# Moving the x tiles ahead in the first loads of a fused attention-and-MLP kernel, and reordering its first Q projection to match

## The chip, the cores and the metric

One core of one Trainium2 chip. The metric is the device time of one execution in microseconds (us); the profile's span, from the first to the last recorded instruction, is about 1.7 us shorter.

## The reference

For `x` of 2048 tokens by 512 dims, the output is `g * a + (1 - g) * b`:

```python
g = sigmoid((x * gate_w).sum(-1))
q, k, v = split(x @ wqkv)            # 32 heads of 16; a: attention over 8 keys, 2 tokens apart
a = softmax(q . k_gathered / 4) @ v_gathered @ wo
b = (gelu(layernorm(x).T @ w1 + b1) @ w2 + b2).T
```

Only the first piece of the projection `x @ wqkv` matters here: Q of the first 512 tokens ("Q block 0"), the first thing that TensorE can do when data arrives.

## The kernel before

The kernel lists its operations, and a static scheduler puts them in an order per engine from its own estimates. Two orders are fixed by hand: that of the loads on each of two DMA queues (the SP queue and the ACT queue), and that of TensorE's operations. Both are touched.

A tile of x is 128 tokens by 512 dims (128 KB). It must be transposed before the projection can use it: TensorE transposes 128 x 128 pieces into PSUM, and VectorE (tiles 0 and 2) or ScalarE (tiles 1 and 3) copies them back. `k_` counts halves of the dims: half 0 is dims 0-255, half 1 is dims 256-511. A block `Wq_dt` holds Wq's 128 rows for dims `128*dt` and up, also 128 KB.

```python
xld = {}
for k_ in (0, 2):
    xld[k_] = xq(k_, "sp")           # load of x tile k_
    xq(k_ + 1, "act")
    wqq(k_, "sp")                    # load of block k_ of Wq
    wqq(k_ + 1, "act")
for k_ in range(2):                  # Wk in two halves, issued when x tile 0 has landed
    load("wk%d" % k_, ..., deps=[xld[0]])
ld_w("wv", 2, 0, 4, "wv")
# ... (cut: x tiles 4-15, small vectors, W1)

PE(f_warm, 2.6, [], ["b7"], "warm")  # 5 matmuls of 512 and 4 of 128 columns on constants

def f_q0(hb, dt):                    # step dt of Q block 0; hb 0: tokens 0-255, 1: 256-511, 2: all 512
    c0, c1 = ((0, 256), (256, 512), (0, 512))[hb]
    # ... (cut: four matmuls, one per bank, accumulating over dt)

def pe_tx(t):                        # transposes of tiles t and t+1
    for k_ in range(2):
        for t_ in (t, t + 1):
            PE(f_tx(t_, k_), ...)    # 2 transposes, then the copy back
            xt_ev(t_, k_)

pe_tx(0)
pe_q0(0, 0)
pe_q0(0, 1)
pe_tx(2)
pe_q0(0, 2)
pe_q0(1, 0)
pe_q0(1, 1)
pe_q0(1, 2)
pe_q0(2, 3)
# ... (cut: the K, V and Q projections, attention, MLP)
```

Of the kernel before, what the change touches and what calls it, by code (L numbers as in the profile page):

```python
# [307 lines left out]
def bass_gated_mix__sliding_local_dilated__mixer_token_mlp__prompt_kernel(nc, A_x, A_wqkv, A_wo, B_x, B_w1, B_b1, B_w2, B_b2, gate_w, out, dbg=None):  # L308
    with contextlib.ExitStack() as es:
# [201 lines left out]
        def ld_first(name, dst, src, nbytes, res, queue):  # L511
            return load(name, dst, src, nbytes, res, queue=queue)

        def xq(t, queue):
            return ld_first("x%d" % t, X[:, t:t + 1, :], xv[:, t:t + 1, :], 131072, ["x%d" % t], queue)

        def wqq(k_, queue):
            return ld_first("wq%d" % k_, WQKV[:, k_:k_ + 1, 0:D], wqkv_v[:, k_:k_ + 1, 0:D], 131072, ["wq%d" % k_], queue)

        xld = {}  # L520
        for k_ in (0, 2):
            xld[k_] = xq(k_, "sp")
            xq(k_ + 1, "act")
            wqq(k_, "sp")
            wqq(k_ + 1, "act")
        for k_ in range(2):
            load("wk%d" % k_, WQKV[:, 2 * k_:2 * k_ + 2, D:2 * D], wqkv_v[:, 2 * k_:2 * k_ + 2, D:2 * D], 2 * 128 * D * 2, ["wk%d" % k_], deps=[xld[0]])
        ld_w("wv", 2, 0, 4, "wv")
# [27 lines left out]
        def PE(fn, dur, reads, writes, name, prio=0):  # L556
            op = A("pe", fn, dur, reads=reads, writes=writes, after=([chain[0]] if chain[0] is not None else []), name=name, prio=prio)
            chain[0] = op
            return op
# [3 lines left out]
        def f_tx(t, k_):  # L563
            def fn(e):
                ins = None
                for d_ in range(2):
                    ins = e.transpose(out=psb(4 + 2 * (t % 2) + k_)[:, d_ * 128:d_ * 128 + 128],  # L567
                                      in_=X[:, t, (2 * k_ + d_) * 128:(2 * k_ + d_ + 1) * 128], identity=IDENT)
                return ins
            return fn  # L570
# [3 lines left out]
        def xt_ev(t, k_):  # L574
            eng = ("dve", "act")[t % 2]
            bk = 4 + 2 * (t % 2) + k_
            src = sub(psb(bk), 0, [(128, 2), (1, 128)])
            dst = sub(XT, 2 * k_ * S + t * 128, [(S, 2), (1, 128)])
            extl[eng] = A(eng, (lambda e: e.tensor_copy(out=dst, in_=src)) if eng == "dve" else act(dst, src, AF.Copy),  # L579
                          0.27 if eng == "dve" else 0.35, reads=["b%d" % bk], writes=["xt0_%d_%d" % (t, k_)], name="ext%d_%d" % (t, k_), prio=-30)  # L580

        def f_q0(hb, dt):
            c0, c1 = ((0, 256), (256, 512), (0, 512))[hb]

            def fn(e):
                ins = None
                for dl in range(4):
                    ins = e.matmul(ps[:, dl, c0:c1], lhsT=sub(WQKV, dt * 3 * D + dl, [(4, 128)]),  # L588
                                   rhs=XT[:, dt, c0:c1], start=(dt == 0 and hb == 0), stop=(dt == 3), skip_group_check=True)
                return ins  # L590
            return fn

        def pe_tx(t):
            for k_ in range(2):
                for t_ in (t, t + 1):
                    PE(f_tx(t_, k_), 0.2, ["x%d" % t_, "ident"], ["b%d" % (4 + 2 * (t_ % 2) + k_)], "tx%d_%d" % (t_, k_))
                    xt_ev(t_, k_)

        def pe_q0(hb, dt):
            PE(f_q0(hb, dt), 0.87 if hb == 2 else 0.44, ["xt0_%d_%d" % (t_, dt // 2) for t_ in ((0, 1), (2, 3), (0, 1, 2, 3))[hb]] + ["wq%d" % dt], ["b%d" % dl for dl in range(4)],  # L600
               "q0_%d_%d" % (hb, dt))
# [3 lines left out]

        pe_tx(0)
        pe_q0(0, 0)
        pe_q0(0, 1)
        pe_tx(2)
        pe_q0(0, 2)  # L610
        pe_q0(1, 0)
        pe_q0(1, 1)
        pe_q0(1, 2)
        pe_q0(2, 3)
        XT0 = ["xt0_%d_%d" % (t, k_) for t in range(4) for k_ in range(2)]

# [402 lines left out]
```

## Time and profile before

| | before |
|---|---|
| median of the first 3 runs | 165.76 us |
| span of the profiled run | 163.9 us |
| TensorE busy | 159.3 us (97%) |
| TensorE in the chain that ended last | 95% |
| first K projection | 9.46 us |
| from there to the end | 154.4 us |

"First K projection" is the start of the first matmul after Q block 0, and it ends what I call the head. Some matmul records are missing from a trace; where that one is, I take the start of its weight load plus the 0.21 us that separate the two elsewhere.

The page of the kernel before, parts 1 and 4: busy time by engine, and the chain of work that ended last, followed back from the last instruction.

```profile
PE 159.3 (97%) x793; PEld 77.5 (47%) x808; DVE 150.7 (92%) x126; ACT 70.2 (43%) x100; POOL 12.0 (7%) x36
...
PE 95%; DMA 2%; ACT 1%; issue 1%; DVE 0%
PE ps L858 29%; PE ps L885 29%; PE ps L649 23%; PE ps L894 8%; PE ps L588 3%; DMA arena<-in_A_x_dram 2%; PE ps L722 1%; ACT arena L453 1%; PE ps L567 1%; PE ps L717 1%; DVE arena L579 0%; PE ps L604 0%
```

TensorE is the chain, and behind the head it has no gaps worth naming. So a change in the head is worth exactly what it moves the first K projection, as long as nothing later is late.

The timeline of the kernel before, TensorE alone, 3 to 10.3 us (start, length, instructions; L551 is the warm-up, L567 the transposes, L588 Q block 0, L649 the projections after it):

```profile
start us, us, engine line op out<-in xcount [idle before <-releaser]
2.51 1.06 PE L551 MATMUL ps<-const-bfloat16-1.0 128*128 128x512 bf16 x5
3.74 1.01 PE L567 MATMUL ps<-arena 128*128 128x128 bf16 x8 [0.17 <-DMA arena<-in_A_x_dram]
4.89 1.61 PE L588 MATMUL ps<-arena 128*128 128x256 bf16 x8
6.33 0.61 PE L567 MATMUL ps<-arena 128*128 128x128 bf16 x8
6.78 2.84 PE L588 MATMUL ps<-arena 128*128 128x256 bf16 x19
9.46 1.03 PE L649 MATMUL ps<-arena 128*128 128x512 bf16 x4
```

Only the first load, x tile 0, makes TensorE wait. The transposes of tiles 2-3 follow the eighth Q matmul without a gap, at 6.33 us; by then their loads have landed. The first eight Q matmuls run slower than the later ones: start to start they are 0.213 us apart until about 6.1 us and 0.110 us after it. That is the clock of TensorE's array going from half to full speed. The Trainium skill ("TensorE: Matmul & The Clock Gate", Part 1) gives N / 1.2 GHz start to start while cold, and the 0.213 us for 256 columns agree.

When each load has landed is read from its semaphore in the trace, which counts to 16 (to 0.01 us). The loads go out in pairs, one on each queue, and land in pairs:

| place | before: SP, ACT | landed, us | after: SP, ACT | landed, us |
|---|---|---|---|---|
| first | x0, x1 | 3.60, 3.80 | x0, x1 | 3.48, 3.67 |
| second | Wq0, Wq1 | 4.25, 4.42 | Wq0, x2 | 4.10, 4.28 |
| third | x2, x3 | 5.91, 6.23 | Wq1, x3 | 6.25, 6.47 |
| fourth | Wq2, Wq3 | 6.65, 6.81 | Wq3, Wq2 | 6.97, 7.18 |

### The profile page before, as it was taken

To read this page: it belongs to the slowest core of one execution; us is meant where nothing else is said; L and a number is where in the kernel's file an instruction comes from. 1 tells how busy PE (TensorE), PEld (TensorE's weight loads), DVE (VectorE), ACT (ScalarE), POOL (GpSimd) and SP (SyncE) were. 2 spreads that over 40 slices of the span, in tenths; PEclk is the share of its full clock that TensorE was granted. 3 is DMA by queue.
4 is the path that set the end of the run, shared out by engine and by line. 5 is a ranking of instruction groups with operands and counts; after the bars stand their busy time and mean duration, and the time that the engine had idled before them with its cause. 6 is when DMAs were issued, how large, how long until landed. Compare 5 with 4: busy or idle time off the path is not lost.

```text
span 163.9 us, 1989 instructions
## 1 busy us (share of the span) xinstructions
PE 159.3 (97%) x793; PEld 77.5 (47%) x808; DVE 150.7 (92%) x126; ACT 70.2 (43%) x100; POOL 12.0 (7%) x36
## 2 busy tenths in 40 slices
PE   7999999999999999999999999999999999999993
PEld 3755555555544444444444344444444444444641
DVE  0589989999999999999999999999999999999971
ACT  3357677766672379753111258111121111111164
POOL 3000021020000000004000000002200222000000
DMA  4999969909499094999998974990998799991014
GB/s 153 288 233 253 254 128 291 199 11 188 91 304 308 1 247 120 256 290 290 298 263 233 270 203 142 298 232 10 283 254 192 185 204 201 211 222 38 32 58 135
DMA packets 44684, 32.24 MB, mean 197 GB/s; under 512 B 7940, under 2 KB 42244, under 8 KB 44676
## 3 DMA queue, kind: packets, MB, share of 16 engines
q1 hardware_dynamic: 41444, 22.06, 51.9%
q0 software_dynamic: 2512, 9.44, 27.2%
q10 hardware_dynamic: 720, 0.62, 1.1%
q8 instruction: 6, 0.10, 0.2%
q14 instruction: 2, 0.02, 0.0%
HBM read 18.88 MB, written 2.10 MB: 128 GB/s over the span
## 4 chain that ended last, share of the span: by engine, by line
PE 95%; DMA 2%; ACT 1%; issue 1%; DVE 0%
PE ps L858 29%; PE ps L885 29%; PE ps L649 23%; PE ps L894 8%; PE ps L588 3%; DMA arena<-in_A_x_dram 2%; PE ps L722 1%; ACT arena L453 1%; PE ps L567 1%; PE ps L717 1%; DVE arena L579 0%; PE ps L604 0%
## 5 line engine op out<-in xcount | busy, mean ns | idle before, releaser
L450 DVE TENSOR_TENSOR arena<-arena 128x4096 bf16<-128x4096 bf16 (+8 forms) x79 | 132.0, 1718 | 1.9 <-ACT arena L453 0.6
L885 PE MATMUL ps<-arena 128*128 128x512 bf16 (+2 forms) x234 | 50.0, 366 | 0.2
L858 PE MATMUL ps<-arena 128*128 128x512 bf16 x218 | 48.5, 379 | 0.3
L453 ACT ACTIVATE arena<-ps,arena 128x512 bf16<-128x512 f32 (+1 forms) x30 | 21.8, 731 | 60.7 <-PE ps L894 37.7
L453 ACT ACTIVATE arena<-ps 128x512 bf16<-128x512 f32 (+3 forms) x53 | 32.9, 629 | 18.3 <-PE ps L649 10.9
L649 PE MATMUL ps<-arena 128*128 128x512 bf16 x173 | 38.0, 379 | 0.2
L885 PEld LDWEIGHTS ps<-arena 128*128 128x128 bf16 x238 | 22.8, 98 | 25.9
L858 PEld LDWEIGHTS ps<-arena 128*128 128x128 bf16 x224 | 21.7, 98 | 26.8 <-issue 0.8
L649 PEld LDWEIGHTS ps<-arena 128*128 128x128 bf16 x176 | 19.9, 113 | 18.0
L894 PE MATMUL ps<-arena 128*128 128x512 bf16 (+2 forms) x67 | 15.6, 366 | 0.1
L453 ACT ACTIVATE arena<-arena 128x16 f32<-128x16 f32 (+5 forms) x10 | 6.7, 678 | 9.7 <-DVE arena L450 9.7
L692 DVE BATCH_NORM_STATS2 arena<-arena 128x6 f32<-128x512 bf16 x16 | 9.9, 679 | 0.5 <-DMA arena<-in_A_x_dram 0.5
L954 ACT ACT_TABLE_LOAD x7 | 9.0, 1283 | 2.8 <-issue 2.7
L894 PEld LDWEIGHTS ps<-arena 128*128 128x128 bf16 x68 | 6.5, 98 | 7.3
L790 POOL DMA_DIRECT2D arena<-arena x8 | 4.3, 556 | 75.2 <-DVE arena L450 75.2
L706 DVE TENSOR_SCALAR arena<-arena 128x512 bf16<-128x512 bf16 x16 | 5.3, 406 | 0.0
L579 DVE COPY arena<-ps 128x256 bf16<-128x256 bf16 x4 | 1.1, 291 | 4.4 <-PE ps L567 4.2
L827 POOL DMA_DIRECT2D arena<-arena x3 | 3.6, 1209 | 17.7 <-DVE arena L450 17.7
L747 POOL DMA_DIRECT2D arena<-arena x2 | 2.5, 1268 | 31.5 <-DVE arena L692 21.5
L588 PE MATMUL ps<-arena 128*128 128x256 bf16 (+1 forms) x27 | 4.4, 313 | 0.2
L588 PEld LDWEIGHTS ps<-arena 128*128 128x128 bf16 x28 | 3.1, 119 | 1.1 <-DVE arena L579 0.4
L551 PE MATMUL ps<-const-bfloat16-1.0 128*128 128x512 bf16 (+1 forms) x9 | 2.7, 483 | 0.8 <-PEq L1004 0.8
(30 smaller groups left out, 14.4 us busy)
## 6 DMA issues: line engine op xcount, KB each, us to landing
arena<-in_B_w_dram SPq DMA_DIRECT2D x7, 1024.0 KB, 6.5
arena<-in_B_w_dram SPq DMA_DIRECT2D x8, 896.0 KB, 9.9
arena<-arena POOLq DMA_DIRECT2D x5, 1024.0 KB, 10.0
arena<-arena POOLq DMA_DIRECT2D x8, 512.0 KB, 11.7
out_dram<-arena SPq DMA_DIRECT2D x15, 128.0 KB, 2.3
arena<-in_A_x_dram SPq DMA_DIRECT2D x3, 512.0 KB, 4.7
arena<-in_A_wqkv_dram SPq DMA_DIRECT2D x2, 256.0 KB, 4.3
arena<-in_A_wqkv_dram SPq DMA_DIRECT2D x1, 512.0 KB, 6.5
```

The source lines that it names most:

```text
L450: return lambda e: e.tensor_tensor(out=o_, in0=a_, in1=b_, op=op_)
L453: return lambda e: e.activation(out=o_, in_=i_, func=f_, **kw)
L588: ins = e.matmul(ps[:, dl, c0:c1], lhsT=sub(WQKV, dt * 3 * D + dl, [(4, 128)]), rhs=XT[:, dt, c0:c1], start=(dt == 0 and hb == 0), stop=(d ...
L649: ins = e.matmul(ps[:, bank, :], lhsT=sub(WQKV, dt * 3 * D + tn * D + dl, [(4, 128)]), rhs=XT[:, dt, sb * 512:(sb + 1) * 512], start=(dt = ...
L692: A("dve", (lambda t_: lambda e: e.bn_stats(out=ST6[:, t_, :], in_=X[:, t_, :]))(t), 0.67, reads=["x%d" % t], writes=["st%d" % t], name="s ...
L706: A("dve", (lambda t_: lambda e: e.tensor_scalar(out=X[:, t_, :], in0=X[:, t_, :], scalar1=col(RSTD, t_), scalar2=col(NMR, t_), op0=ALU.mu ...
L790: prev = sch.dma("pool", (lambda d_, s_: lambda e: e.dma_start(d_, s_))(dst, src), 524288, sch.dsem("av%d_%d" % (h, c)), issue=1.0, reads= ...
L827: sch.dma("pool", (lambda o_, i_: lambda e: e.dma_start(o_, i_, accum_op=ALU.add, max_dma_last_dim=4096))(pw(0, 4), pw(4, 4)), 1800000, sc ...
L858: ins = e.matmul(ps[:, bank, :], lhsT=W1H[ft // 2][:, st, 128 * (ft % 2):128 * (ft % 2) + 128], rhs=X[:, st, :], start=(st == 0), stop=(st ...
L885: ins = e.matmul(ps[:, bank, 0:c1 - c0], lhsT=W2S[i // 2][:, ft, 128 * (i % 2):128 * (i % 2) + 128], rhs=UT[:, ft, c0:c1], start=(ft == 0) ...
L894: ins = e.matmul(ps[:, bank, 0:c1 - c0], lhsT=OT[:, i // 2, dl, 128 * (i % 2):128 * (i % 2) + 128], rhs=WO[:, dl, c0:c1], start=False, sto ...
L954: e.preload_act_table_set(want)
```

## The change

The intent is to have the x tiles early, so that the transposes of tiles 2-3 can follow Wq0's first step at once, and to do the last two steps (dims 256-511) in one go for all 512 tokens, with wider and fewer matmuls.

```diff
         xld = {}
-        for k_ in (0, 2):
-            xld[k_] = xq(k_, "sp")
-            xq(k_ + 1, "act")
+        for k_ in range(4):
+            xld[k_] = xq(k_, "sp" if k_ == 0 else "act")
+        for k_ in (0, 1, 3):
             wqq(k_, "sp")
-            wqq(k_ + 1, "act")
+        wqq(2, "act")
...
         pe_tx(0)
         pe_q0(0, 0)
+        pe_tx(2)
         pe_q0(0, 1)
-        pe_tx(2)
-        pe_q0(0, 2)
         pe_q0(1, 0)
         pe_q0(1, 1)
-        pe_q0(1, 2)
+        pe_q0(2, 2)
         pe_q0(2, 3)
```

## The prediction

> **What bounds the kernel.** TensorE. In the chain that ended last PE is 95%, unbroken from 3.74 us (first transpose, released by x tile 0) to about 160.4 us. VectorE (92%) follows PE's start: its first long product waits for a K eviction. It finishes its last attention output at 158.7 us and PE uses that from 159.35 us (timeline): about 0.6 us of room. So a change in the head is worth what it moves the first K projection, now at 9.46 us.
>
> **The head now** (timeline and landings by semaphore). x0 lands at 3.61, x1 3.80, Wq0 4.25, Wq1 4.43, x2 5.91, x3 6.23, Wq2 6.65, Wq3 6.81, Wk0 7.46 us. PE: transposes of tiles 0-1 3.74 to about 4.55; a hole of about 0.35 us for the evictions (DVE 0.29, ACT 0.38 us); eight 256-column matmuls from 4.90, the first five or six at 213 ns start to start, later ones at 110; transposes of tiles 2-3 from 6.34 at 56 ns each; then sixteen 256-column matmuls, with one hole of about 0.07 us for an eviction; four of 512 at 216 ns. The 213 ns are the half clock: the Trainium skill, "TensorE: Matmul & The Clock Gate", Part 1, gives exactly N/1.2 GHz start to start when cold, and says the window is free-running. This trace agrees (256/1.2 = 213), with the change at about 6.05 us.
>
> **What the change does.** Matmuls: 24 of 256 and 4 of 512 columns become 16 and 8. Eight steps of 110 ns become four of 216, a saving of 0.02 us. Transposes, evictions and bytes are unchanged.
>
> Loads: by place in the two queues, only x2 and Wq1 swap (second against third), and Wq2 and Wq3 (fourth). The Trainium skill, "DMA: Bandwidth & Descriptors", "Issuing engines are not separate DMA queues", says that the queues share the same 16 engines; the near-equal landings of each pair agree. So I expect x2 at about 4.4, Wq1 at 5.9, but x3 still third on its queue, at about 6.2, and Wq2/Wq3 at 6.7-6.8.
>
> PE order: Wq1's first step used to fill the time until x3; now it stands behind the transposes of tiles 2-3. My estimate from these times: first step to 5.75 (cold), transposes of x2 to 5.96, then a hole of about 0.3 us until x3 at 6.25; transposes to 6.6; Wq1's two half steps to about 7.9 with no eviction hole; two 512-column steps to about 9.65. That is about 0.1-0.2 us later than 9.46. If x3 lands near 5.1 (14 of its 16 parts did), the change gains about 0.2-0.3 us instead. The clock's phase moves this by up to some 0.3 us.
>
> **Prediction.** 165.8 us (before 165.76), range 165.2 to 166.5. Faster by over 2%: 0.01; within 2%: 0.98; slower by over 2%: 0.01. Removing every hole in the head would be under 0.5%.
>
> **What would show it.** First K projection at 9.2 to 9.9 us; x2 landing near 4.4, x3 near 6.2; an idle stretch before tile 3's first transposes, released by the x load; the 0.07 us eviction hole gone; L588 with 16 matmuls of 256 and 8 of 512; the rest as long as before (about 154.4 us).
>
> **What would make it wrong.** x3 landing far earlier or later than its place in the queue says; the clock staying at half through the new hole; the kernel's static scheduler, which orders every engine from its own estimates, moving the group sums or VectorE's additions; noise (165.38 and 165.76 before).

## More of the kernel before

The kernel before had one run of 225.62 us, the first of all, which the ratios leave out.

Splitting the execution at the first K projection (busy us per engine; then the granted clock, DMA share and GB/s):

```profile
0.00:9.46 9.46, 8.25 (x52) 5.52 (x54) 3.68 (x9) 2.71 (x5) 1.55 (x23) 1.00 0.73 232
9.46:163.90 154.44, 151.05 (x742) 71.93 (x754) 147.04 (x118) 67.46 (x95) 10.48 (x13) 1.00 0.81 195
```

## The result, and the profile after

| | before | after |
|---|---|---|
| median of 6 runs | 165.46 us (the 225.62 among them) | 165.93 us (165.22 to 166.12) |
| ratio | | 1.002, 95% interval 0.9998 to 1.0043 |
| profiled span | 163.9 us | 164.4 us |
| first K projection | 9.46 us | 9.97 us |
| from there to the end | 154.4 us | 154.4 us |

A ratio is the mean time of one kernel's fast runs over that of the other's of the same rounds, so it is not quite the ratio of the medians quoted.

The page of the kernel after, the same parts as shown of before (its lines below the edit are numbered one lower):

```profile
PE 159.1 (97%) x789; PEld 76.9 (47%) x804; DVE 150.8 (92%) x126; ACT 70.2 (43%) x100; POOL 12.0 (7%) x36
...
PE 93%; DMA 3%; ACT 1%; issue 1%; ACTq 1%
PE ps L857 29%; PE ps L884 29%; PE ps L648 23%; PE ps L893 8%; DMA arena<-in_A_x_dram 3%; PE ps L588 2%; PE ps L721 1%; ACT arena L453 1%; PE ps L716 1%; ACTq L494 1%; PE ps L567 0%; PE ps L604 0%
```

A load of x has grown from 2% to 3% of the chain: it now reaches to 6.46 us instead of 3.60. The pairs landed at 3.48, 3.67 (x0, x1), 4.10, 4.28 (Wq0, x2), 6.25, 6.47 (Wq1, x3) and 6.97, 7.18 us (Wq3, Wq2). The timeline of the kernel after, TensorE alone, same window:

```profile
start us, us, engine line op out<-in xcount [idle before <-releaser]
2.51 1.06 PE L551 MATMUL ps<-const-bfloat16-1.0 128*128 128x512 bf16 x5
3.62 1.01 PE L567 MATMUL ps<-arena 128*128 128x128 bf16 x8
4.77 0.84 PE L588 MATMUL ps<-arena 128*128 128x256 bf16 x4
5.44 0.28 PE L567 MATMUL ps<-arena 128*128 128x128 bf16 x2
6.51 0.51 PE L567 MATMUL ps<-arena 128*128 128x128 bf16 x6 [0.80 <-DMA arena<-in_A_x_dram]
6.86 3.27 PE L588 MATMUL ps<-arena 128*128 128x256 bf16 x20
```

The hole stands in the fifth row: two transposes of tile 2 are done, then TensorE waits 0.80 us for tile 3. The clock turned early in this execution, at about 5.3 us, which gave some of it back beforehand. The split of the kernel after at its first K projection:

```profile
0.00:9.97 9.97, 8.14 (x49) 5.00 (x51) 3.83 (x9) 2.71 (x5) 1.55 (x23) 1.00 0.76 230
9.97:164.40 154.43, 150.99 (x741) 71.88 (x754) 146.97 (x117) 67.45 (x95) 10.49 (x13) 1.00 0.81 194
```

The rest is the same 154.4 us, so the whole difference of the two profiles, 0.5 us, is in the head. Why did tile 3 land later than its place says? The DMA view of the first 12 us shows a slump, in slices of 0.3 us (first line: busy share of the 16 DMA engines in tenths, 9 is 90% or more). Before:

```profile
DMA  0000000499999999779999989897889999999681
GB/s 0 0 0 0 0 0 24 31 314 379 383 376 362 324 284 222 212 253 307 301 331 328 328 304 331 287 263 256 297 277 338 369 387 355 324 216 160 108 84 42
```

After:

```profile
DMA  0000003499999973599999999996989999999979
GB/s 0 0 0 0 0 0 113 89 314 359 369 359 253 181 96 126 164 328 335 369 359 355 379 372 362 307 232 208 236 283 311 335 357 339 318 248 224 165 140 93
```

Both have a slump while the third pair is under way: from 4.5 to 5.4 us before, down to 212 GB/s, and from 3.6 to 5.1 us after, down to 96 GB/s. In it some packets of 1 KB, which mostly take 0.046 us, took up to 0.8 us before and up to 1.4 us after. They are not the whole of it: the DMA engines were also partly idle, in three slices of after (70, 30 and 50% busy) and two of before (70%). Why is not shown.

### The profile page after: what moved, and what is told of

Same layout as the page of the kernel before. It is cut to its first block, busy times and chain, and to the rows that moved or that the text cites. A ratio compares the mean times of both kernels' runs of the same rounds, so it can differ in the third digit from the quotient of the medians.

```text
span 164.4 us, 1981 instructions
## 1 busy us (share of the span) xinstructions
PE 159.1 (97%) x789; PEld 76.9 (47%) x804; DVE 150.8 (92%) x126; ACT 70.2 (43%) x100; POOL 12.0 (7%) x36
## 4 chain that ended last, share of the span: by engine, by line
PE 93%; DMA 3%; ACT 1%; issue 1%; ACTq 1%
PE ps L857 29%; PE ps L884 29%; PE ps L648 23%; PE ps L893 8%; DMA arena<-in_A_x_dram 3%; PE ps L588 2%; PE ps L721 1%; ACT arena L453 1%; PE ps L716 1%; ACTq L494 1%; PE ps L567 0%; PE ps L604 0%
## 5 line engine op out<-in xcount | busy, mean ns | idle before, releaser
L884 PEld LDWEIGHTS ps<-arena 128*128 128x128 bf16 x238 | 22.8, 98 | 25.9
L857 PEld LDWEIGHTS ps<-arena 128*128 128x128 bf16 x224 | 21.7, 98 | 26.9 <-issue 0.8
L648 PEld LDWEIGHTS ps<-arena 128*128 128x128 bf16 x176 | 19.9, 113 | 18.0
L893 PEld LDWEIGHTS ps<-arena 128*128 128x128 bf16 x68 | 6.5, 98 | 7.3
```

The source lines that it names most:

```text
L648: ins = e.matmul(ps[:, bank, :], lhsT=sub(WQKV, dt * 3 * D + tn * D + dl, [(4, 128)]), rhs=XT[:, dt, sb * 512:(sb + 1) * 512], start=(dt = ...
L857: ins = e.matmul(ps[:, bank, :], lhsT=W1H[ft // 2][:, st, 128 * (ft % 2):128 * (ft % 2) + 128], rhs=X[:, st, :], start=(st == 0), stop=(st ...
L884: ins = e.matmul(ps[:, bank, 0:c1 - c0], lhsT=W2S[i // 2][:, ft, 128 * (i % 2):128 * (i % 2) + 128], rhs=UT[:, ft, c0:c1], start=(ft == 0) ...
L893: ins = e.matmul(ps[:, bank, 0:c1 - c0], lhsT=OT[:, i // 2, dl, 128 * (i % 2):128 * (i % 2) + 128], rhs=WO[:, dl, c0:c1], start=False, sto ...
```

## The experiments

The theory: **the head ends when the last load that TensorE has to wait for lands, plus the TensorE work that still stands behind it.** Call that load's landing L and the work W. In the kernel after, TensorE waits for x3, and W is 9.97 - 6.47 = 3.5 us. For the kernel before, the expectations below take 9.46 - 6.23 = 3.2 us, as if it had waited for x3 too. Its timeline shows that it did not: x3 landed at 6.23, TensorE was busy with Q matmuls, most of them at half clock, until 6.33, and began tile 3's transposes at 6.45. So that 3.2 is no W. What compares is the work from tile 3's first transpose on: 9.46 - 6.45 = 3.0 us before and 9.97 - 6.51 = 3.5 us after. The change puts the four matmuls of Wq1's first step (0.44 us), which used to run ahead of tile 3, behind it.

Rival A: the small difference is noise and the clock's phase. Rival B: the new load order itself brings tile 3 later. Each kernel had one profiled run and 5 timed ones, each on one chip with its own runs of before.

The profiles in one table, without e5, e7 and e11, which change more than the two orders (us; "landed" is the last load that TensorE waited for after tiles 0-1, "turn" is when the clock went to full, from the spacing of the matmuls and, where the trace has one, its record of the clock granted to TensorE):

| run | landed | first K projection | difference | turn | rest | span |
|---|---|---|---|---|---|---|
| before | no wait | 9.46 | | 6.1 | 154.4 | 163.9 |
| e4 (old orders, Wk held) | Wq2 6.40 | 9.10 | 2.7 | 5.7 | 154.9 | 164.0 |
| e9 (old orders) | Wq2 6.66 | 9.35 | 2.7 | 5.2 | 154.4 | 163.7 |
| after | x3 6.47 | 9.97 | 3.5 | 5.3 | 154.4 | 164.4 |
| c1 (the change again) | x3 6.38 | 9.88 | 3.5 | 4.1 | 154.4 | 164.3 |
| e2 (old loads, new TensorE order) | x3 5.57 | 9.07 | 3.5 | 4.7 | 154.4 | 163.5 |
| e3 (change, Wk held) | x3 5.50 | 9.00 | 3.5 | 5.1 | 154.7 | 163.7 |
| e6 (x3 fourth) | x3 6.14 | 9.64 | 3.5 | 5.8 | 154.4 | 164.0 |
| e1 (new loads, old TensorE order) | no wait | 9.47 | | 6.2 | 154.4 | 163.9 |
| e8 (before, filled) | no wait | 9.76 | | 6.8 | 154.4 | 164.2 |
| e10 (old orders) | no wait | 9.29 | | 6.1 | 154.4 | 163.7 |

With the new TensorE order all five here waited for x3, and the sum holds to 0.01 us. With the old one only e4 (by 0.02 us) and e9 waited, last for Wq2, with 2.7 us of work behind it. In the other four TensorE came to tiles 2-3 after their loads, and the first K projection followed tile 2's first transpose by 3.1 us (3.3 in e8, where the clock had not turned yet).

### e1 and e2: each half of the change alone

e1 takes the first hunk of the diff alone (loads), e2 the second alone (TensorE order).

> The new load order with the old TensorE order. Theory (last needed load of the third pair sets the head: first K projection starts when that load lands plus the TensorE work still standing behind it): here Wq1 and x3 are third; behind them stand 4 matmuls of Wq1, 8 transposes, 16 matmuls of 256 and 4 of 512 columns, about 3.6 us at full clock against about 3.2 in before (9.46 - 6.23); so with a landing at 6.2 to 6.5 us the first K projection is at 9.8 to 10.1 us, and the time 0.3 to 0.5 us over before. Rival A (the small loss is only noise or the phase of the clock): the first K projection at 9.3 to 9.6 us and the ratio 1.000 within 0.001, hole or no hole. Rival B (the loss is all in the load order): as slow as the change, ratio about 1.002, while the order alone (e2) costs nothing.

> The old load order with the new TensorE order. Theory: x2 and x3 are the third pair; behind them stand 8 transposes, 12 matmuls of 256 and 8 of 512 columns, about 3.55 us; so with a landing at 5.9 to 6.3 us there is an idle stretch of 0.3 to 0.9 us before tile 2's transposes and the first K projection is at 9.5 to 9.9 us, time 0.2 to 0.4 us over before. Rival A: as before, ratio 1.000 within 0.001. Rival B: as before, because the loads are.

e1 gave 165.77 us against 165.70 before, ratio 1.0028 (0.9995 to 1.0062; one of its runs, 167.62, carries most of that). e2 gave 165.59 us, ratio 0.9998 (0.9982 to 1.0014). In time alone neither half differs from before. The profiles say more. TensorE in e2:

```profile
4.77 0.60 PE L588 MATMUL ps<-arena 128*128 128x256 bf16 x4
5.35 0.78 PE L567 MATMUL ps<-arena 128*128 128x128 bf16 x8
5.97 3.27 PE L588 MATMUL ps<-arena 128*128 128x256 bf16 x20
9.29 1.03 PE L648 MATMUL ps<-arena 128*128 128x512 bf16 x4
```

(The record of the first K matmul, at 9.07, is missing.) x3 landed at 5.57 and the K projection came 3.50 us later, the W of the change. It is early, and outside the expected 9.5 to 9.9, because this execution's loads were early; the clock had turned at 4.7 us. TensorE in e1:

```profile
4.84 1.67 PE L588 MATMUL ps<-arena 128*128 128x256 bf16 x8
6.35 0.61 PE L567 MATMUL ps<-arena 128*128 128x128 bf16 x8
6.79 2.84 PE L588 MATMUL ps<-arena 128*128 128x256 bf16 x19
```

There is no wait for a load: the clock stayed at half until 6.2 us, and Wq1 (5.35) and x3 (5.59) had landed by the time TensorE came to them. So the theory's sum for e1 (9.8 to 10.1) missed: TensorE's own work at half clock was what ended last.

In time, rival B fares best of the three: it expected about 1.002 for the loads and nothing for the order, though both intervals hold 1. The landings do not support it: x3, third on its queue in either load order, landed at 5.43 to 6.47 us (mean 5.87) in the five profiles with the new loads and at 5.57 to 6.23 (mean 5.91) in the six with the old.

### e3 and e4: do the Wk loads cause the slump?

Both hold the Wk loads back, e3 in the change (until x3), e4 in before (until x2):

```diff
-            load("wk%d" % k_, ..., deps=[xld[0]])
+            load("wk%d" % k_, ..., deps=[xld[3]])     # e3; in e4 xld[2]
```

> The change with the Wk loads (and what is queued behind them) issued only when x3 has landed, not x0. It asks whether the long DMA packets at 3.7 to 5.1 us (up to 1.4 us instead of 0.05) come from the Wk and Wv loads being issued then. If they do: no packet over 0.3 us before x3 lands, x3 at 5.0 to 5.4 us, the hole ahead of tile 3's transposes under 0.2 us, and either the first K projection at 8.6 to 9.1 us or, if Wk then comes late, a new wait on Wk at 8.6 to 9.5 us. If the stall is something else: x3 again at 6.2 to 6.5 us, and Wk late too, landing at about 9.5 to 10.5 us, so the time 0 to 0.8 us over the change.

> Before with the Wk loads issued only when x2 has landed. Same question on the old order: if the Wk loads cause the late landings, x2 and x3 land by 5.1 us rather than 5.9 and 6.2, and the first K projection is 0 to 0.4 us earlier than before unless it waits for Wk; if not, x2 and x3 land at 5.8 to 6.3 us again and K waits for Wk, 0 to 0.8 us later than before.

e3: 166.15 us, ratio 1.0041 (1.001 to 1.0072). e4: 166.24 us, ratio 1.0042 (1.0027 to 1.0058). Packets of 0.3 to 0.64 us were there at 3.4 to 4.4 us in both, when no Wk load had been issued, so Wk is not what makes these. x3 landed at 5.50 and 5.91 us, earlier than in the unheld pair, but e1 and e2 had 5.59 and 5.57 without holding anything. What causes the long packets stays open; the trace does not say to which load a packet belongs.

Both kernels show something else: their first K projections are early (9.00 and 9.10), yet they are slower on average. (The profiled execution is the fastest of the six in both, so the profiles show the loss only in part.) Their rest is 154.7 and 154.9 us instead of 154.4. The waits of e4, 20 to 26 us, TensorE:

```profile
PE ps L649 <- DMA arena<-in_A_x_dram: 0.3, 1, 0.3
```

The later loads of x stand behind Wk on the SP queue and had been pushed back with it; the chain of e4 runs through that queue's issues from 5.7 us on and ends in a load of x that TensorE waited for until 24.29 us. That load landed at 24.16 us, 1.06 later than in before, and the next matmul started 0.72 us after the one ahead of it instead of 0.22: this is the 0.5 us. In e3 TensorE waits at the same place, until 24.00 us, 0.3 us longer than usual: the load landed at 23.86 us, and an eviction by ScalarE, which the profile names, ended at 23.90. So 14 us later e4 lost more than it had gained in the head (0.5 against 0.36 us), and e3 a part of it.

### c1: the change once more

> The change once more, for a second profile and another mean beside before. Theory: first K projection = landing of x3 (or Wq1, if later by more than the transposes take) + 3.50 us, the rest 154.4 us; x3 lands anywhere in 5.4 to 6.5 us, as the long DMA packets fall on another load; ratio to before 1.000 to 1.003. Rival A (noise only): ratio 0.999 to 1.001 and no fixed sum. Rival B (this load order itself draws the stall): x3 again over 6.2 us, ratio over 1.002.

165.75 us against 165.42 before, ratio 1.0009 (0.998 to 1.0039), with one run of 168.14 us left out as slow (its granted clock was 0.99). The profile:

```profile
5.14 0.28 PE L567 MATMUL ps<-arena 128*128 128x128 bf16 x2
6.43 0.51 PE L567 MATMUL ps<-arena 128*128 128x128 bf16 x6 [1.02 <-DMA arena<-in_A_x_dram]
6.77 3.27 PE L588 MATMUL ps<-arena 128*128 128x256 bf16 x20
9.88 1.46 PE L648 MATMUL ps<-arena 128*128 128x512 bf16 x6
```

The clock turned as early as 4.1 us here, amid the transposes, and TensorE reached the hole 0.3 us sooner than in the first profile; the hole was simply longer. x3 at 6.38 plus 3.50 is 9.88. The early clock was worth nothing here, where a load was the limit. (That x3 is again over 6.2 us is what rival B expected; the ratio over 1.002 is not there.)

### e6: tile 3 one place later

The edit, condensed:

```diff
-            xld[k_] = xq(k_, "sp" if k_ == 0 else "act")      # ACT: x1, x2, x3, Wq2
+            # ACT: x1, x2, Wq2, x3
```

> The change with x3 and Wq2 exchanged on their queue: x3 is fourth. Dose: x3 lands 0.4 to 0.7 us later than a third place, at 6.1 to 6.9 us, the hole ahead of tile 3's transposes grows to 0.8 to 1.3 us, the first K projection is again landing + 3.50, at 9.6 to 10.4 us; time 0.3 to 0.6 us over the change, ratio to before 1.003 to 1.006. If the hole is not what sets the head, the time stays at the change's.

166.54 us, ratio 1.0078 (1.0035 to 1.0122): slower than before, clear of noise, and over the expected 1.003 to 1.006. Two of its runs took 167.16 and 168.07 us (see e5); the other four alone would give 1.0047. In the profile x3 landed at 6.14, 0.77 us after the Wq2 ahead of it, and the K projection came 3.50 us later, so the sum holds. But the profile does not show the larger dose: the third pair of this execution was early (5.18 and 5.37 us), x3 landed before the 6.47 and 6.38 of the third place in after and c1, the hole was only about 0.3 us, and the run (165.75) is one of the two fastest of the six. That the later place is what made the others slow is likely, but not shown.

### e5: all four x tiles in the first two places

The edit, condensed:

```diff
+        for k_ in (0, 2): xld[k_] = xq(k_, "sp"); xq(k_ + 1, "act")
+        for k_ in (0, 2): wqq(k_, "sp"); wqq(k_ + 1, "act")
...
+        pe_tx(0); pe_tx(2)
+        for dt_ in range(4): pe_q0(2, dt_)       # sixteen matmuls of 512 columns
+        # and start=True for step 0 of hb 2 as well
```

> All four x tiles in the first two places of both queues, the Wq blocks behind; all eight tile transposes first, then Q in sixteen matmuls of 512 columns. The eviction hole of 0.35 us after the first transposes is filled, but all of Q stands behind the third pair (Wq0, Wq1): landing of Wq0 at 5.4 to 6.2 us + about 3.5 us gives the first K projection at 8.9 to 9.7 us; the clock should turn fast later, if transposes with idle around them count less. Ratio 0.999 to 1.003 by the theory; rival A gives 1.000 within 0.001.

165.79 us, ratio 1.0044 (1.0008 to 1.0079). This is the intent of the change taken to its end, and it is slower than before. Its profile fell on a run of 167.31 us:

```profile
3.60 1.95 PE L568 MATMUL ps<-arena 128*128 128x128 bf16 x16
6.03 5.33 PE L589 MATMUL ps<-arena 128*128 128x512 bf16 x16 [0.48 <-ACT arena L453]
11.19 1.03 PE L645 MATMUL ps<-arena 128*128 128x512 bf16 x4
```

Sixteen matmuls took 5.33 us instead of the 3.5 that 0.216 us each would give: the clock stayed at half until 9.5 us, about 3.4 us after the turns of before and e1 (6.1 and 6.2). The first K projection came at 11.19, far outside the expected 8.9 to 9.7. 3.4 us is the length of the clock's window that the Trainium skill gives ("TensorE: Matmul & The Clock Gate", Part 1). The trace's record of the granted clock agrees: full speed lasted 157.013 us in e5 and e10 and 160.426 us in after and c1, and the difference is 3.413. e10's clock turned at 6.12 us and e5's at 9.52, one such window later. So this execution fits one window that did not count as busy, with 0.48 us of idle time in it ahead of the first Q matmul, waiting for Wq0 (landed at 5.89 us) and for a copy by ScalarE that ended 0.09 us after it. That is one profile, not a proof. Runs over 167 us occurred 6 times in the 42 executions of the kernels that have the x tiles ahead (after, c1, e1, e3, e5, e6, e11), and in none of the 74 of the others, the 225.62 aside. Only e5's was profiled, so whether the other five are the same thing stays open.

### e7: least work behind the last load

x2 and Wq2 go third, x3 and Wq3 fourth; TensorE does tile 2, Wq2's step on tiles 0-1, tile 3, Wq3's step on tiles 0-1, then tiles 2-3 in four steps.

> A version meant to have the least work behind the last load: x2 and Wq2 third, x3 and Wq3 fourth; tiles 0-1 with Wq0, Wq1 and Wq2, then tile 3's transposes, Wq3's step on tiles 0-1 to cover the eviction, then tiles 2-3 in four 256-column steps. Behind x3 stand 4 transposes and 20 matmuls of 256 columns, about 2.45 us: landing at 6.0 to 6.8 us gives the first K projection at 8.5 to 9.3 us where the clock turned early; with a late clock 9.3 to 9.5 as in before. Ratio to before 0.996 to 1.000. If rival A holds, 1.000 within 0.001.

165.29 us against 165.42, ratio 1.0007 (0.998 to 1.0035): nothing gained. In the profile the slump fell on the third pair again (x2 at 6.40), and TensorE waited 0.72 us for it; x3 landed at 7.07, just as TensorE came to it, and the K projection started at 9.73, 2.7 us later. The smaller W was paid for by a later L, and tile 3's copy still left a hole of about 0.18 us. This was the candidate to beat both kernels, and it does not.

### e8 and e11: filling the idle stretches with dummy matmuls

```diff
-            for n_ in (512,) * 5 + (128,) * 4:
+            for n_ in (512,) * 5 + (128,) * 6:
...
         pe_tx(0)
+        fill(3, 128, 3)          # three matmuls on constants
         pe_q0(0, 0)
+        fill(7, 512, 2)          # e11 alone: two ahead of pe_tx(2)
```

> Before with dummy matmuls in its two early idle stretches: two more of 128 columns at the end of the warm-up, three of 128 in the eviction hole after the first transposes. In ten profiles the clock turned full at 4.1 to 6.2 us, once at 9.5. If a busier TensorE makes it turn earlier, the turn is at 4 to 5.5 us and the first K projection at 8.7 to 9.3 us, ratio to before 0.996 to 0.999; if the turn depends on the phase of the window alone, the ratio is 0.999 to 1.002 and the turn anywhere in 4.1 to 6.2 us.

> The change with the same fillers as e8, and two dummy matmuls of 512 columns in the hole ahead of the transposes of tiles 2-3. The hole is a wait for a load, so filling it cannot bring the first K projection under landing of x3 + 3.50: ratio 1.000 to 1.003 to before, as the change. If the hole's harm is through the clock (half speed through it), filling gives 0.998 to 1.000 and none of the runs over 167 us that the kernels with this hole show now and then (6 of about 36, none of before's 22).

e8: 165.57 against 165.43, ratio 1.0005 (0.9984 to 1.0026). Its clock turned at 6.8 us, later than in any profile but e5's and outside both ranges of the expectation. In this profile a TensorE with less idle time did not turn the clock earlier. e11: 165.67, ratio 1.0021 (1.0 to 1.0043), as the change; filling the hole does not remove it. None of e11's six runs was over 167 us (highest 166.39), which at a rate of one in seven says little. Its profile had x3 at 5.43 and no hole, so there the filler only cost time.

### e9 and e10: do transposes count for the clock?

The nine warm-up matmuls of before are replaced by eighteen of 128 columns, as transposes (e9) or plain matmuls (e10), on the same operands, from 1.43 us on.

> Before with its warm-up (nine matmuls from 0.85 us) replaced by eighteen transposes of 128 columns of a constant from about 1.5 us. If transposes do not count as activity for the clock, the clock turns only after a stretch of real matmuls, at 7 to 9.6 us, and the first K projection is at 10 to 11 us, ratio 1.004 to 1.010 to before and well over e10. If they count like matmuls, it equals e10 within 0.001.

> The control of e9: eighteen plain matmuls of 128 columns from about 1.5 us in place of the transposes, the same times and operands. The clock turns at 4.5 to 7.5 us; first K projection 9.0 to 9.9 us; ratio to before 1.000 to 1.003.

e9: 165.55 us, ratio 1.0012 (0.9995 to 1.0029). e10: 165.70 us, ratio 1.0016 (0.9997 to 1.0035). They are equal within the noise. TensorE in e9:

```profile
1.43 2.10 PE L551 MATMUL ps<-arena,const-bfloat16-1.0 128*128 128x128 bf16 x18 [1.43 <-POOL arena L460]
3.44 1.03 PE L567 MATMUL ps<-arena 128*128 128x128 bf16 x8
4.62 1.29 PE L588 MATMUL ps<-arena 128*128 128x256 bf16 x8
5.98 0.72 PE L567 MATMUL ps<-arena 128*128 128x128 bf16 x8
6.71 2.80 PE L588 MATMUL ps<-arena 128*128 128x256 bf16 x20
9.35 1.03 PE L649 MATMUL ps<-arena 128*128 128x512 bf16 x4
```

Nothing but transposes ran until 4.62 us, and the clock was full at about 5.2 us, within the third real matmul. So transposes count here, and they alone do not explain the late clock of e5. The last three lines show what an earlier clock does to the old orders: TensorE now waits for x2, x3 and Wq2 (landed at 5.93, 6.15 and 6.66 us), and the first K projection gains only 0.11 us on before's.

## Why the prediction was right

**The sum.** 165.8 us was predicted and 165.93 measured, within the range. The mechanism was right: a hole ahead of tile 3's transposes, released by the load of x. Three terms were off:

- *The landing of x3* was put at "about 6.2"; it was 6.47 in the profiled run. Over the profiles with x3 in third place of its queue it was anywhere from 5.43 to 6.47, whatever the load order, and the DMA slump differed from one profile to the next. One trace of before had given one draw of a lottery.
- *The hole* was put at "about 0.3 us"; it was 0.80. Of the extra 0.5 us about 0.2 us is the landing and the rest is that TensorE came to it earlier: x0 had landed 0.12 us sooner than before, and the clock turned at about 5.3 us and not 6.1.
- *"Wq1's two half steps ... with no eviction hole"* was wrong. The hole of about 0.07 us is there in the change as before. Wq1's first half step was to cover the copy of tile 3, but this copy started at 6.83 us, 0.32 us after tile 3's first transpose, and took 0.38.

The first K projection came at 9.97 us, just outside the "9.2 to 9.9" that the prediction gave for it and 0.32 us after the 9.65 of its sum. These errors add up: 0.22 us is the later landing (6.47 against 6.25), 0.10 us the work behind it (3.50 against 3.40), most of it the eviction hole. That the median still fell within 0.13 us is partly luck: the profiled run is the slowest of the six, and the prediction started from 165.76, where six runs of before give 165.46. It foresaw a rise of 0.04 us; by the ratio it was about 0.3. (The prediction also misread one thing: 13, not 14, of x3's 16 parts had landed by 5.1 us.)

**Where the expected gain went.** The change saves four matmuls and four weight loads, but 256 columns take half of 512, so nothing is saved in time (0.02 us). It would fill the early eviction hole only if tiles 2 and 3 were there by 4.5 us. Tile 2 was, at 4.28; tile 3 was not, and the transposes are in order. In exchange, Wq1's first step, which had covered the wait, went behind it. The two profiles differ by 0.51 us at the first K projection: tile 3's transposes began 0.06 us later (6.51 against 6.45), and 0.45 us more work stood behind them. Before spent the time up to x3's landing on Wq1's first step at half clock; after spent it waiting.

**Shown and not shown.** That W is 3.5 behind x3 for the new TensorE order is shown in five profiles. For the old order no profile was set by x3; the 2.7 us behind Wq2 rest on two. That the whole span follows the first K projection is shown by the rest of 154.4 us in every profile but the two that held Wk. A loss in time of the change itself is not shown: its two ratios, 1.002 and 1.0009, both have 1 in their interval. Rival A holds to that extent: single executions of before spread over 0.7 to 1.3 us on one chip, more than the effect. The larger dose (e6) and the extreme (e5) do lose clear of noise, but e6's profile does not show why, and e5's shows a late clock.

**The static scheduler.** It moved one long VectorE product four places behind four statistics instructions, and no new wait of TensorE came of it. The prediction had named this as a risk.

## What to carry to other kernels

When an in-order engine waits for loads at the start, write down for each order the landing of the last load it must wait for and the work that stands behind it; their sum decides if the engine gets there before the load does (here before did not), and moving a load one place up does nothing if the work that covered the wait moves behind it. Read landings from several profiles before building on one: here x3 in the same place landed anywhere within 1 us. A later load pushed back to help the first ones can return as a wait far down the kernel (e4, and in part e3).

## What the Trainium skill lacked or had wrong

- "TensorE: Matmul & The Clock Gate", Part 4, says that the full clock does not engage for transposes, as they do not count as busy in the same way. In e9 only transposes ran until 4.62 us and the clock was full at about 5.2 us, as with plain matmuls (e10, about 6.1 us, within the spread). In c1 the turn came in the middle of the transposes: start to start they went from 0.107 to 0.056 us at 4.1 us. (The profile lists transposes as MATMUL; that they ran in the page's transpose mode is taken from the kernel's call.)
- The same page, Part 1, puts the turn at around 4 us into sustained activity, within 0.5 us from run to run. In 13 of 14 profiles it came between 4.1 and 6.8 us, which is 3.3 to 6.0 us after the first matmul, and in one (e5) at 9.5 us, 8.7 us after it. The page's own advice not to fit to a cold count agrees with that.
- No page that I read tells of single packets of 1 KB that take ten to thirty times the usual 0.046 us: the longest of the first 12 us took between 0.48 (e9) and 1.58 us (e6) in each of the 14 profiles. "DMA: Bandwidth & Descriptors" speaks of memory latency under load only in general. In before and after they fall in the slump ahead of the third pair of loads (which landed at 5.2 to 6.6 us over all profiles); that they set this landing is not shown.
